# A gated recurrence with an MLP behind it: softplus and erf from their own tables in place of five table passes and a Newton step

## The chip, the cores and the metric

The kernel runs on one core of a Trainium2 chip. The metric is the device time of one execution in microseconds. Five engines work side by side, each from its own queue in order: TensorE (PE, with its weight loads listed as PEld), VectorE (DVE), ScalarE (ACT), GpSimd (POOL) and SyncE (SP, which issues the DMAs). All arithmetic is in float32.

## The reference

The core of it (4 x 8 heads, 768 steps, head size 48; then 3072 tokens, width 384, hidden width 2048):

```python
mag = np.sqrt(a_re * a_re + a_im * a_im)
scale = np.minimum(mag, 0.999) / (mag + 1e-06)
a_re_n, a_im_n = (a_re * scale, a_im * scale)
for t in range(S):
    ar, ai = (a_re_n[:, :, t, :, None], a_im_n[:, :, t, :, None])
    new_re = ar * S_re - ai * S_im
    new_im = ar * S_im + ai * S_re
    S_re, S_im = (new_re + kv, new_im)          # kv = outer(k_t, v_t)
    y[:, :, t] = np.einsum('bhd,bhde->bhe', q[:, :, t], S_re)
...
h = x @ w_in
sp = np.maximum(h, 0.0) + np.log1p(np.exp(-np.abs(h)))
g = h * erf(sp)
return (g @ w_out)
```

The weights w_in and w_out come as float64 and are narrowed on the chip.

## The kernel before, in words

The 3072 tokens are cut into 12 units of 256 tokens, two chunks of 128 each. The main loop runs u = 0 to 12. In round u four strands are emitted interleaved by `weave`, each over its own share of the round:

- **rec**: the recurrence of unit u, chunk 0 then chunk 1. The 8 heads go as two groups of 4 (hg 0 and 1). Decays, keys and queries are transposed (tiles r, k, q into PSUM tr, and on to rT, K, Q in SBUF); dg is the diagonal; then seven levels of doubling (L384 to L402). At each level and head group 4 products go into PSUM tile lv (in the trace 8 PE instructions, since a float32 product shows as two), DVE copies a part of lv into A (L389) and multiplies a half of Q by decays (L398), POOL does the same for a half of K (L400). The next level of that group needs Q and K. Two PSUM buffers serve lv. At the end of a chunk come kn, y and kv (the output and the new state), and xt, the transpose of the output into xT.
- **dec** (gate_decay): the decay r of unit u+1, a chain of 15 DVE instructions on 128 x 768 elements or more with a reciprocal (L267) in it and Square, Ln, Exp and Abs on ACT; emitted over the first fifth of the round. **ang** (gate_angle): Arctan, running sums (PSUM tile sum) and Sin, late in the round.
- **ffs**: the MLP of unit u-1, in two slabs of 8 blocks of 128 hidden features. `ff_in` puts two blocks at a time (6 products) into a PSUM tile hps of 128 x 512, of which there are two buffers. ACT copies it to h (L477) and DVE clamps it to z (L480). `softplus` makes four ACT passes over the 128 x 2048 slab: Exp, Ln(1 + .), then Ln and Exp(-.), the last two for 1 / z in tile yy. `erf_times_h` goes by quarters of 512: two DVE instructions for a Newton step on yy (L505, L506), Gelu on ACT, and two DVE instructions that turn gelu(sqrt(2) z) into h * erf(z) (L508, L509). `ff_out` sums 16 products per chunk of 128 tokens into PSUM tile ops (L519), ACT scales the result, and it goes out.
- weights, in round 0 alone.

Round 12 has only ffs. Round 11 has no dec and no ang. So rounds 1 to 10 are alike, and round 0 is the start.

What sets the order on each engine is a scheduler that goes by the emission order as priority and by its own estimate of the engines' time; buffers come from pools. `act` chains all table functions in the order of emission, and puts a table load where the next function is in another set; plain copies on ACT are outside of that chain. A PSUM tile that two engines read is read by one after the other, in the order of emission.

Of the kernel before, what the change touches and what calls it, by code (L numbers as in the profile page):

```python
# [18 lines left out]
P = 128  # L19
# [6 lines left out]
    "gelu_and_others": (AF.Gelu,),  # L26
# [4 lines left out]
def weave(*streams):  # L31
    """Emit the steps of each (begin, end, steps) evenly over its part of the window."""
    order = []
    for si, (begin, end, steps) in enumerate(streams):
        for i, step in enumerate(steps):
            order.append((begin + (end - begin) * (i + 0.5) / len(steps), si, i, step))
    for _, _, _, step in sorted(order, key=lambda e: e[:3]):
        step()
# [3 lines left out]
def kernel(  # L42
# [11 lines left out]
    """Gated linear recurrence with complex diagonal gates, then h * erf(softplus(h)) between two  # L54
    matrix products, in float32 throughout.

    A gate is r * exp(2 pi i theta). The angles enter the queries and keys once, as cosine and sine
    of their running sum (kept within half a turn), which leaves a real recurrence with decay r over
    2 * D rows. A chunk of 128 steps is solved by seven levels of doubling: at the level of blocks of
    m steps, a query in the second block of a pair meets the keys of the first, the query times the  # L60
    decays from its block's start up to it, the key times those after it up to its block's end.
    These are products of decays only, never quotients, so gates may be as small as they like,
    or zero.
    """
# [15 lines left out]
    RT2 = math.sqrt(2.0)  # L80
# [12 lines left out]
    yp = ctx.enter_context(tc.tile_pool(name="yp", bufs=1))  # L93
# [21 lines left out]
    # pair[l]: 1 where the key of the row lies in the first block of the pair of blocks of 2**l  # L115
    # whose second block the query of the column lies in.
# [58 lines left out]
    def narrow(dst, src, shape):  # L175
        """float64 from memory, as raw 64-bit words, to the nearest float32: the upper 20 bits of the
        significand with the exponent's bias changed, and the lower 32 as a number scaled by the
        power of two, added. What is under float32's normal range becomes zero."""
# [21 lines left out]
    def weights():  # L200
        """Steps that bring the weights on chip."""
# [19 lines left out]
    def gate_decay(u):  # L221
# [6 lines left out]
        def s0():  # L228
# [4 lines left out]
            # The logarithm's range; below it the decay is under 1e-13 in any case.  # L233
# [8 lines left out]
        def s2():  # L242
            # One Newton step takes 1 / sqrt(s) to full precision.
# [10 lines left out]
        def s3():  # L254
            # mag in s; 1 / ((mag + EPS) * (mag + |ar|)) in y
# [27 lines left out]
    def gate_angle(u):  # L283
        def t0():
            ar = flat(T["ar", u])
            n, hv = T["n"], T["hv"]
            # Half the angle of (|ar|, ai); turns of (ar, ai) from it.
# [174 lines left out]
    def ff_in(u, sl):  # L462
# [4 lines left out]
        def two(i):  # L467
            def f():
# [3 lines left out]
                for e in range(2):  # L472
                    f0 = (sl * SLAB + i + e) * P
                    for kd in range(KD):
                        nc.tensor.matmul(out=ps[:, e, :], lhsT=w_in_sb[:, kd, f0:f0 + P], rhs=T["xT", u][:, kd, :],  # L475
                                         start=(kd == 0), stop=(kd == KD - 1))
                nc.scalar.copy(out=T["h", u, sl][:, i:i + 2, :], in_=ps)  # L477
                # Above 8, erf(softplus(h)) is 1 in float32; below -16, 1 + exp(h) is 1 to its last place.
                # h itself stays whole.
                nc.vector.tensor_scalar(out=T["z", u, sl][:, i:i + 2, :], in0=ps, scalar1=8.0, scalar2=-16.0,  # L480
                                        op0=OP.min, op1=OP.max)
# [3 lines left out]
    def softplus(u, sl):  # L485
        def f():
            z = T["z", u, sl]
            y = yp.tile([P, SLAB, NT], FP, tag="yy", name="yy")
            act(out=z, in_=z, func=AF.Exp)
            act(out=z, in_=z, func=AF.Ln, bias=1.0)  # L490
            act(out=y, in_=z, func=AF.Ln)
            act(out=y, in_=y, func=AF.Exp, scale=-1.0)
            T["yy", u, sl] = y
        return [f]

    def erf_times_h(u, sl):
        # erf(z) = sqrt(2) * gelu(sqrt(2) * z) / z - 1; a Newton step gives -1 / z to full precision.
        n = SLAB // 4

        def part(i):  # L500
            def f():
                ss = slice(i * n, (i + 1) * n)
                h, z, y = (T[nm, u, sl][:, ss, :] for nm in ("h", "z", "yy"))
                t = yp.tile([P, n, NT], FP, tag="t", name="t")
                nc.vector.tensor_tensor(out=t, in0=z, in1=y, op=OP.mult)  # L505
                nc.vector.scalar_tensor_tensor(out=y, in0=t, scalar=-2.0, in1=y, op0=OP.add, op1=OP.mult)  # L506
                act(out=z, in_=z, func=AF.Gelu, scale=RT2)
                nc.vector.tensor_tensor(out=z, in0=z, in1=y, op=OP.mult)  # L508
                nc.vector.scalar_tensor_tensor(out=h, in0=z, scalar=1.0 / RT2, in1=h, op0=OP.add, op1=OP.mult)  # L509
            return f  # L510
        return [part(i) for i in range(SLAB // n)]
# [66 lines left out]
```

## Time and profile before

| | |
|---|---|
| time, median of 2 runs (lowest to highest) | 1558.42 us (1557.83 to 1559.02) |
| span of the profiled execution | 1557.6 us |
| PE busy | 1350.9 us (87%) |
| DVE busy | 1171.2 us (75%) |
| ACT busy | 597.6 us (38%) |
| POOL busy | 418.0 us (27%) |
| mean granted TensorE clock | 0.814 |

The profiled execution's own span is 0.8 us below the median of the runs. The granted clock is given as a share of 2.4 GHz; 0.5 is 1.2 GHz, and a mean between the two says which part of the stretch stood at each. An engine's idle time is listed with what ended it.

### The profile page before, as it was taken

How to read it: one execution, taken by the hardware profiler on the slowest of the kernel's cores; microseconds unless marked ns; L12 is line 12 of the kernel's file. 1: busy time of each engine (PE TensorE's matmuls, PEld its weight loads, DVE VectorE, ACT ScalarE, POOL GpSimd, SP SyncE). 2: the span in 40 equal slices, each digit the busy share in tenths (PEclk: the TensorE clock that was granted, in tenths of full speed). 3: DMA queues.
4: the chain of work that ended last, by engine and by line, in shares of the span. 5: the costliest groups of instructions: out<-in, count | busy, mean ns of one | idle time of the engine just before them, and what ended most of it. 6: DMA issues, size and time to landing. Idle time of an engine off the chain costs nothing.

```text
span 1557.6 us, 18736 instructions
## 1 busy us (share of the span) xinstructions
PE 1350.9 (87%) x6912; PEld 1137.9 (73%) x6912; DVE 1171.2 (75%) x2104; ACT 597.6 (38%) x751; POOL 418.0 (27%) x387
## 2 busy tenths in 40 slices
PE   0455598998998998998998998998998998999997
PEld 0244477887877787787877787887877887888784
DVE  6999979579579669579589669579589669578535
ACT  2301033443443443444443443434443443434425
POOL 4445523122123222122132222122132122132210
PEclk9997557797797886797797887797797887799888
DMA  8214100100100100100100100100100100000000
GB/s 173 90 31 114 58 11 11 31 21 11 32 21 11 31 21 11 31 21 11 32 21 11 31 21 11 31 21 11 31 21 10 31 21 0 1 11 1 0 11 10
DMA packets 131386, 42.09 MB, mean 27 GB/s; under 512 B 125408, under 2 KB 128480, under 8 KB 130528
## 3 DMA queue, kind: packets, MB, share of 16 engines
q1 hardware_dynamic: 131296, 40.90, 11.4%
q8 instruction: 55, 0.90, 0.2%
q14 instruction: 35, 0.29, 0.1%
HBM read 36.18 MB, written 4.72 MB: 26 GB/s over the span
## 4 chain that ended last, share of the span: by engine, by line
PE 60%; DVE 25%; issue 6%; ACT 6%; POOL 2%; DMA 0%; SPq 0%; DVEq 0%; ACTq 0%; POOLq 0%
PE lv L384 20%; PE ops L519 12%; PE hps L475 9%; PE y L411 4%; DVE y L267 3%; PE y L414 3%; PE tr L340 3%; PE kv L429 3%; ACT z L146 2%; DVE A L389 2%; PE dg L370 2%; DVE tot L402 2%; DVE z L480 2%; DVE Q L398 1%; POOL K L400 1%
## 5 line engine op out<-in xcount | busy, mean ns | idle before, releaser
L384 PEld LDWEIGHTS lv<-Q,K 96*128 96x128 f32 x2688 | 438.3, 246 | 158.9 <-issue 100.6
L384 PE MATMUL lv<-Q,K 96*128 96x64 f32 x2688 | 448.6, 330 | 101.5 <-DVE Q L398 90.7
L400 POOL TENSOR_TENSOR K<-K,tot 96x256 f32<-96x256 f32 x280 | 262.7, 939 | 377.0 <-PE lv L384 243.8
L475 PE MATMUL hps<-xT,w_in_sb 128*128 128x256 f32 x1152 | 305.5, 415 | 0.6 <-ACT xT L449 0.6
L519 PE MATMUL ops<-w_out_sb,h 128*128 128x384 f32 x768 | 283.6, 498 | 7.8 <-DVE z L480 6.5
L146 ACT ACTIVATE z<-z 128x2048 f32<-128x2048 f32 (+1 forms) x144 | 152.3, 1057 | 319.9 <-DVE t L505 308.6
L475 PEld LDWEIGHTS hps<-xT,w_in_sb 128*128 128x128 f32 x1152 | 232.8, 212 | 32.2 <-ACT xT L449 1.0
L400 POOL TENSOR_TENSOR K<-K,rT 96x256 f32<-96x256 f32 x48 | 74.1, 1544 | 640.5 <-PE lv L384 640.5
L389 DVE COPY_PREDICATED A<-pair,lv 128x256 f32<-128x256 uint8 x336 | 171.3, 510 | 42.1 <-PE lv L384 39.4
L519 PEld LDWEIGHTS ops<-w_out_sb,h 128*128 128x128 f32 x768 | 135.1, 192 | 71.1 <-DVE z L480 6.9
L398 DVE TENSOR_TENSOR Q<-Q,tot 96x256 f32<-96x256 f32 x280 | 150.2, 536 | 0.0
L477 ACT COPY h<-hps 128x512 f32<-128x512 f32 x96 | 55.8, 581 | 161.0 <-PE hps L475 161.0
L437 DVE TENSOR_TENSOR S<-S,kv 96x192 f32<-96x192 f32 x32 | 11.2, 350 | 133.1 <-PE kv L429 133.1
L480 DVE TENSOR_SCALAR z<-hps 128x512 f32<-128x512 f32 x96 | 65.0, 682 | 44.1 <-ACT h L477 44.1
L411 PE MATMUL y<-v,A 128*128 128x48 f32 x384 | 95.3, 354 | 0.2 <-DVE tot L402 0.2
L411 PEld LDWEIGHTS y<-v,A 128*128 128x128 f32 x384 | 84.3, 279 | 0.4 <-DVE tot L402 0.4
L426 ACT COPY kn<-kn 128x384 f32<-128x384 f32 x40 | 19.2, 479 | 165.6 <-PE kn L424 146.3
L340 PE MATMUL tr<-ident,r 128*96 128x128 f32 x192 | 49.5, 387 | 37.3 <-DVE r L278 36.5
L414 PE MATMUL y<-S,Q 96*128 96x48 f32 x320 | 81.4, 347 | 0.0
L145 ACT ACT_TABLE_LOAD x62 | 79.5, 1283 | 1.1
L505 DVE TENSOR_TENSOR t<-z,yy 128x512 f32<-128x512 f32 x96 | 71.7, 747 | 9.7 <-ACT yy L146 9.7
L506 DVE SCALAR_TENSOR_TENSOR yy<-t,yy 128x512 f32<-128x512 f32 x96 | 74.7, 778 | 0.1
(96 smaller groups left out, 1753.6 us busy)
## 6 DMA issues: line engine op xcount, KB each, us to landing
raw<-in_moe_w_in_dram SPq DMA_DIRECT2D x6, 1024.0 KB, 5.5
raw<-in_moe_w_out_dram SPq DMA_DIRECT2D x8, 768.0 KB, 4.3
ar<-in_a_re_dram SPq DMA_DIRECT2D x24, 192.0 KB, 3.2
ai<-in_a_im_dram SPq DMA_DIRECT2D x24, 192.0 KB, 3.2
q<-in_q_dram SPq DMA_DIRECT2D x24, 192.0 KB, 3.7
k<-in_k_dram SPq DMA_DIRECT2D x24, 192.0 KB, 3.3
v<-in_v_dram SPq DMA_DIRECT2D x24, 192.0 KB, 3.2
out_dram<-o SPq DMA_DIRECT2D x24, 192.0 KB, 1.9
```

What stands on the lines that cost most here:

```text
L145: in_order(nc.scalar.preload_act_table_set(sets[0]))
L146: in_order(nc.scalar.activation(func=func, **kw))
L340: nc.tensor.transpose(out=ps[0:D2, j, :], in_=src(j), identity=ident)
L384: nc.tensor.matmul(out=lv[:, j], lhsT=K[0:D2, j, :], rhs=Qv[0:D2, j, :, 1, :], start=True, stop=True)
L389: nc.vector.copy_predicated(out=halves(A, 1), mask=pair[l], data=lv.rearrange("p h b m -> p (h b) m"))
L398: nc.vector.tensor_tensor(out=halves(Q, 1)[0:D2], in0=halves(Q, 1)[0:D2], in1=over(0), op=OP.mult)
L400: nc.gpsimd.tensor_tensor(out=halves(K, 0)[0:D2], in0=halves(K, 0)[0:D2], in1=over(1), op=OP.mult)
L411: nc.tensor.matmul(out=y[:, j, :], lhsT=st["A"][:, j, :], rhs=T["v", u][:, c, hg * HG + j, :], start=True, stop=first)
L414: nc.tensor.matmul(out=y[:, j, :], lhsT=st["Q"][0:D2, j, :], rhs=T["S", hg][0:D2, j, :], start=False, stop=True)
L475: nc.tensor.matmul(out=ps[:, e, :], lhsT=w_in_sb[:, kd, f0:f0 + P], rhs=T["xT", u][:, kd, :], start=(kd == 0), stop=(kd == KD - 1))
L480: nc.vector.tensor_scalar(out=T["z", u, sl][:, i:i + 2, :], in0=ps, scalar1=8.0, scalar2=-16.0, op0=OP.min, op1=OP.max)
L519: nc.tensor.matmul(out=ps, lhsT=T["h", u, sl][:, e, jj * P:(jj + 1) * P], rhs=w_out_sb[:, i, :], start=(i == 0), stop=(i == KF - 1))
```

## The change

Softplus and Erf each have a table. hps is now copied to h by DVE, and ACT makes z = Softplus(hps) from PSUM at once, in pieces of 512. One Erf pass goes over the slab of 2048, and four DVE multiplications of 512 give h * erf(z). The clamp, the tile yy, the four slab passes, the Gelu and the Newton step are gone, and so is the scale in `ff_out`. Softplus and Erf stand in two different table sets. The line numbers of the changed kernel are lower by 1 up to its L476.

```diff
-    "gelu_and_others": (AF.Gelu,),
+    "softplus": (AF.Softplus,),
+    "sigmoid_and_others": (AF.Erf,),
...
-                nc.scalar.copy(out=T["h", u, sl][:, i:i + 2, :], in_=ps)
-                nc.vector.tensor_scalar(out=T["z", u, sl][:, i:i + 2, :], in0=ps, scalar1=8.0, scalar2=-16.0,
-                                        op0=OP.min, op1=OP.max)
+                nc.vector.tensor_copy(out=T["h", u, sl][:, i:i + 2, :], in_=ps)
+                act(out=T["z", u, sl][:, i:i + 2, :], in_=ps, func=AF.Softplus)
...
-    def softplus(u, sl):
-        def f():
-            z = T["z", u, sl]
-            y = yp.tile([P, SLAB, NT], FP, tag="yy", name="yy")
-            act(out=z, in_=z, func=AF.Exp)
-            act(out=z, in_=z, func=AF.Ln, bias=1.0)
-            act(out=y, in_=z, func=AF.Ln)
-            act(out=y, in_=y, func=AF.Exp, scale=-1.0)
...
     def erf_times_h(u, sl):
-                t = yp.tile([P, n, NT], FP, tag="t", name="t")
-                nc.vector.tensor_tensor(out=t, in0=z, in1=y, op=OP.mult)
-                nc.vector.scalar_tensor_tensor(out=y, in0=t, scalar=-2.0, in1=y, op0=OP.add, op1=OP.mult)
-                act(out=z, in_=z, func=AF.Gelu, scale=RT2)
-                nc.vector.tensor_tensor(out=z, in0=z, in1=y, op=OP.mult)
-                nc.vector.scalar_tensor_tensor(out=h, in0=z, scalar=1.0 / RT2, in1=h, op0=OP.add, op1=OP.mult)
+            h, z = T["h", u, sl], T["z", u, sl]
+            act(out=z, in_=z, func=AF.Erf)
+            for i in range(0, SLAB, 2):
+                nc.vector.tensor_tensor(out=h[:, i:i + 2, :], in0=h[:, i:i + 2, :], in1=z[:, i:i + 2, :], op=OP.mult)
...
-                nc.scalar.mul(out=o, in_=ps, mul=-RT2)
+                nc.scalar.copy(out=o, in_=ps)
...
-                ffs += ff_in(u - 1, sl) + softplus(u - 1, sl) + erf_times_h(u - 1, sl)
+                ffs += ff_in(u - 1, sl) + erf_times_h(u - 1, sl)
```

With fewer steps in ffs the emission is spread anew, and the scheduler's order changes. PE before, in chunk 0 of a round from the first level on (hps are the products of `ff_in`, lv those of the levels, 4 to a level and head group):

```order
L384 MATMUL lv<-Q,K 128x64 x4
L475 MATMUL hps<-xT,w_in_sb 128x256 x3
L384 MATMUL lv<-Q,K 128x64 x4
L475 MATMUL hps<-xT,w_in_sb 128x256 x7
L384 MATMUL lv<-Q,K 128x64 x48
L424 MATMUL kn<-ident,K 128x96 x6
```

PE now, from the same place:

```order
L383 MATMUL lv<-Q,K 128x64 x4
L474 MATMUL hps<-xT,w_in_sb 128x256 x3
L383 MATMUL lv<-Q,K 128x64 x8
L474 MATMUL hps<-xT,w_in_sb 128x256 x5
L383 MATMUL lv<-Q,K 128x64 x4
L474 MATMUL hps<-xT,w_in_sb 128x256 x7
L383 MATMUL lv<-Q,K 128x64 x8
L474 MATMUL hps<-xT,w_in_sb 128x256
L383 MATMUL lv<-Q,K 128x64 x8
L474 MATMUL hps<-xT,w_in_sb 128x256 x2
L383 MATMUL lv<-Q,K 128x64 x4
L474 MATMUL hps<-xT,w_in_sb 128x256
```

Before, 36 of the round's 48 hps products stand ahead of the last six levels, which run as one block of 48 lv, and 6 follow it in the chunk. Now 30 stand ahead of level 2 and 14 are spread from there to the end of the chunk; 4 are left for chunk 1 (before: 6).

ACT before, around the same place (s, y, n are gate_decay's, q the transposed query, h the copy of hps):

```order
L145 ACT_TABLE_LOAD
L477 COPY h<-hps 128x512
L146 ACTIVATE y<-s 128x768
L146 ACTIVATE y<-y 128x768
L146 ACTIVATE n<-y 128x768
L477 COPY h<-hps 128x512
L354 COPY K<-tr 96x512
L361 COPY q_4073<-tr 96x512
L477 COPY h<-hps 128x512
L146 ACTIVATE n<-ar 128x768
L361 COPY q_4091<-tr 96x512
L477 COPY h<-hps 128x512 x2
```

ACT now (z<-hps is Softplus, z<-z is Erf):

```order
L145 ACTIVATE z<-hps 128x512
L144 ACT_TABLE_LOAD
L145 ACTIVATE y<-s 128x768
L360 COPY q_3878<-tr 96x512
L145 ACTIVATE y<-y 128x768
L145 ACTIVATE n<-y 128x768
L360 COPY q_3896<-tr 96x512
L145 ACTIVATE n<-ar 128x768
L144 ACT_TABLE_LOAD
L145 ACTIVATE z<-hps 128x512 x3
L144 ACT_TABLE_LOAD
L145 ACTIVATE z<-z 128x2048
```

The first Softplus now stands ahead of gate_decay's Ln and the second behind its Abs, with a table load on each side. In the whole program there are 83 table loads now and 63 before; a round of the middle has 7 instead of 5.

DVE now, at gate_decay's reciprocal (before, the clamp of one hps stood just ahead of the reciprocal, and both head groups' level-0 instructions just behind it):

```order
L261 TENSOR_TENSOR hv<-hv,ai 128x768
L266 RECIPROCAL y<-y 128x768
L476 COPY h<-hps 128x512
L270 TENSOR_TENSOR hv<-hv,y 128x768
L271 TENSOR_TENSOR n<-n,y 128x768
L272 SCALAR_TENSOR_TENSOR s<-s 128x768
L388 COPY_PREDICATED A<-pair_130,lv 128x128x2
L277 TENSOR_TENSOR r<-s,n 128x1536
L397 TENSOR_TENSOR Q<-Q,tot 96x128x2
```

The level-0 instructions have moved ahead of the reciprocal, and a copy of hps stands right behind it. In both kernels level 1's Q, on which PE's level 2 waits, comes behind r.

## Rows read from the trace of the kernel before

**Rows 1.** The page: busy time per engine, and the granted clock in 40 slices.

```profile
PE 1350.9 (87%) x6912; PEld 1137.9 (73%) x6912; DVE 1171.2 (75%) x2104; ACT 597.6 (38%) x751; POOL 418.0 (27%) x387
PEclk9997557797797886797797887797797887799888
```

**Rows 2.** Windows of one round; length, busy PE, PEld, DVE, ACT, POOL, clock.

```profile
807.00:831.00 24.00, 23.70 (x126) 20.26 (x125) 19.64 (x30) 14.36 (x22) 2.29 (x2) 0.93 0.17 33
831.00:840.00 9.00, 2.33 (x19) 2.15 (x18) 9.00 (x12) 7.36 (x5) 3.27 (x2) 0.72 0.00 1
840.00:869.00 29.00, 28.52 (x130) 26.91 (x131) 21.05 (x42) 5.93 (x10) 7.29 (x10) 0.50 0.00 1
869.00:917.00 48.00, 47.66 (x270) 36.29 (x268) 36.79 (x77) 19.51 (x24) 15.91 (x14) 1.00 0.15 34
```

**Rows 3.** PE in order of time, same round: start, length, what, idle before.

```profile
827.86 3.24 PE L475 MATMUL hps<-xT,w_in_sb 128*128 128x256 f32 x14
833.17 1.99 PE L384 MATMUL lv<-Q,K 96*128 96x64 f32 x16 [2.08 <-DVE Q L398]
839.75 18.77 PE L384 MATMUL lv<-Q,K 96*128 96x64 f32 x80 [4.59 <-DVE Q L398]
...
865.31 2.04 PE L475 MATMUL hps<-xT,w_in_sb 128*128 128x256 f32 x4
...
870.53 0.49 PE L448 MATMUL xt<-ident,x 128*128 128x128 f32 x3
```

**Rows 4.** DVE in order of time, same round.

```profile
816.41 0.95 DVE L247 TENSOR_TENSOR n<-n,s 128x768 f32<-128x768 f32 x1
...
827.25 4.93 DVE L267 RECIPROCAL y<-y 128x768 f32<-128x768 f32 x1
...
837.50 1.77 DVE L278 TENSOR_TENSOR r<-s,n 128x1536 f32<-128x1536 f32 x1
```

**Rows 5.** Groups of instructions by line and shape: busy, mean ns, idle before.

```profile
L506 DVE SCALAR_TENSOR_TENSOR yy<-t,yy 128x512 f32<-128x512 f32 x96 | 74.7, 778 | 0.1
L508 DVE TENSOR_TENSOR z<-z,yy 128x512 f32<-128x512 f32 x96 | 70.3, 732 | 0.2
L509 DVE SCALAR_TENSOR_TENSOR h<-z,h 128x512 f32<-128x512 f32 x96 | 69.0, 719 | 0.1
L480 DVE TENSOR_SCALAR z<-hps 128x512 f32<-128x512 f32 x96 | 65.0, 682 | 44.1 <-ACT h L477 44.1
L146 ACT ACTIVATE z<-z 128x2048 f32<-128x2048 f32 x48 | 91.7, 1911 | 11.2 <-DVE z L480 10.8
L146 ACT ACTIVATE z<-z 128x512 f32<-128x512 f32 x96 | 60.5, 630 | 308.8 <-DVE t L505 308.6
L145 ACT ACT_TABLE_LOAD x62 | 79.5, 1283 | 1.1
```

**Rows 6.** ACT in order of time: a pass and the table load behind it.

```profile
835.20 1.91 ACT L146 ACTIVATE yy<-yy 128x2048 f32<-128x2048 f32 x1
837.12 1.28 ACT L145 ACT_TABLE_LOAD   x1
```

**Rows 7.** Round 11, which has no gate_decay: windows, then PE.

```profile
1412.00:1438.00 26.00, 22.14 (x154) 20.09 (x153) 22.97 (x42) 14.93 (x15) 10.45 (x14) 0.96 0.00 1
1438.00:1451.00 13.00, 13.00 (x66) 12.73 (x67) 4.52 (x12) 2.64 (x6) 0.00 (x0) 0.50 0.01 1
...
1428.48 2.38 PE L475 MATMUL hps<-xT,w_in_sb 128*128 128x256 f32 x10
...
1434.42 0.55 PE L424 MATMUL kn<-ident,K 96*128 96x96 f32 x4 [1.72 <-POOL K L400]
```

**Rows 8.** Round 12, the tail: PE.

```profile
1498.44 23.72 PE L475 MATMUL hps<-xT,w_in_sb 128*128 128x256 f32 x96 [0.57 <-ACT xT L449]
1528.65 13.59 PE L519 MATMUL ops<-w_out_sb,h 128*128 128x384 f32 x32 [6.49 <-DVE z L480]
1543.54 10.67 PE L519 MATMUL ops<-w_out_sb,h 128*128 128x384 f32 x32 [1.31 <-DVE h L509]
```

More of the change, by code (lines that the diff above doesn't have):

```diff
@@ L79 @@
     NSL = KF // SLAB
-    RT2 = math.sqrt(2.0)
     const = ctx.enter_context(tc.tile_pool(name="const", bufs=1))
@@ L92 @@
     zp = ctx.enter_context(tc.tile_pool(name="zp", bufs=2))
-    yp = ctx.enter_context(tc.tile_pool(name="yp", bufs=1))
     op = ctx.enter_context(tc.tile_pool(name="op", bufs=2))
@@ L476, in f, with erf_times_h @@
                                          start=(kd == 0), stop=(kd == KD - 1))
-                nc.scalar.copy(out=T["h", u, sl][:, i:i + 2, :], in_=ps)
-                nc.vector.tensor_scalar(out=T["z", u, sl][:, i:i + 2, :], in0=ps, scalar1=8.0, scalar2=-16.0,
-                                        op0=OP.min, op1=OP.max)
+                nc.vector.tensor_copy(out=T["h", u, sl][:, i:i + 2, :], in_=ps)
+                act(out=T["z", u, sl][:, i:i + 2, :], in_=ps, func=AF.Softplus)
             return f
         return [two(i) for i in range(0, SLAB, 2)]
-    def softplus(u, sl):
+    def erf_times_h(u, sl):
         def f():
-            z = T["z", u, sl]
-            y = yp.tile([P, SLAB, NT], FP, tag="yy", name="yy")
-            act(out=z, in_=z, func=AF.Exp)
-            act(out=z, in_=z, func=AF.Ln, bias=1.0)
-            act(out=y, in_=z, func=AF.Ln)
-            act(out=y, in_=y, func=AF.Exp, scale=-1.0)
-            T["yy", u, sl] = y
-        return [f]
-    def erf_times_h(u, sl):
-        n = SLAB // 4
-        def part(i):
-            def f():
-                ss = slice(i * n, (i + 1) * n)
-                h, z, y = (T[nm, u, sl][:, ss, :] for nm in ("h", "z", "yy"))
-                t = yp.tile([P, n, NT], FP, tag="t", name="t")
-                nc.vector.tensor_tensor(out=t, in0=z, in1=y, op=OP.mult)
-                nc.vector.scalar_tensor_tensor(out=y, in0=t, scalar=-2.0, in1=y, op0=OP.add, op1=OP.mult)
-                act(out=z, in_=z, func=AF.Gelu, scale=RT2)
-                nc.vector.tensor_tensor(out=z, in0=z, in1=y, op=OP.mult)
-                nc.vector.scalar_tensor_tensor(out=h, in0=z, scalar=1.0 / RT2, in1=h, op0=OP.add, op1=OP.mult)
-            return f
-        return [part(i) for i in range(SLAB // n)]
+            h, z = T["h", u, sl], T["z", u, sl]
+            act(out=z, in_=z, func=AF.Erf)
+            for i in range(0, SLAB, 2):
+                nc.vector.tensor_tensor(out=h[:, i:i + 2, :], in0=h[:, i:i + 2, :], in1=z[:, i:i + 2, :], op=OP.mult)
+        return [f]
     def ff_out(u):
```

## The prediction

> **What bounds the kernel now.** I read the page's busy row and clock row first, then windows over one middle round, then PE and DVE in order of time inside it. PE is busy for 87% of the span and DVE for 75%, but the clock row does not stay at 9: after the start it swings between 6 and 9 in each round [rows 1]. So time can be won in three ways: less PE idle time, more time at 2.4 GHz, or less PE work. The change takes no product away, so only the first two are open.
>
> The windows of the round that runs from 807 to 923 us show where both are lost [rows 2]. From 831 to 840 PE is busy for 2.33 of 9.00 us while DVE is busy for all 9.00. From 840 to 869 PE is busy for 28.52 of 29.00 us, but at a clock of 0.50. From 869 to 917 it is busy for 47.66 of 48.00 at 1.00: there PE alone is the limit, and a freer DVE buys nothing. In order of time [rows 3]: the last block of hps products ends at 831.1, PE waits 2.08 and then 4.59 us for Q from DVE, and when the levels go on at 839.75 they run 80 lv instructions in 18.77 us, 0.235 us each. Just ahead of the second wait, 16 took 1.99, 0.124 each. The clock comes back by 869, 3.7 us after hps products start again at 865.31. What holds DVE is gate_decay: from n (816.41) over the reciprocal (4.93 us) to the end of r (839.27) it goes through a queue of 22.9 us [rows 4], and Q of level 1 stands behind r.
>
> So a round of 116 us holds about 7 us of PE waiting and about 29 us at half the clock, which cost some 14 us more. Ten rounds (1 to 10) are like this.
>
> **The change, part by part.**
>
> *DVE work taken out.* The clamp (682 ns) becomes a copy of the same shape from PSUM, at the same price. The final instruction stays as a multiplication, which I price as the 732 ns row. Three of the five others go or shrink: 778 + 732 + 719 ns less per quarter [rows 5] is 2.23 us, 8 quarters to a round, 17.8 us a round and 214 us over the 24 slabs. Nearly all of it lay beside a busy PE (from 840 on, 21.05 us of DVE work in 29 us that PE filled), so I put its direct worth at nothing in the middle rounds. Its cover is PE at the low clock; were PE at 2.4 GHz there, the old DVE work would be in the way (below).
>
> *ACT.* Per slab four passes of 1911 ns and four Gelus of 630 become four Softplus of 512 and one Erf. No row shows a Softplus or an Erf; the bounds are the nearest passes, 630 ns for 512 elements and 1911 for 2048, and I take these. 20 more table loads of 1283 ns are 26 us. ACT is at 38% and ends below 30%: off the path but for two places. First, gate_decay's Ln now waits for the first Softplus and a load. The Softplus itself waits for DVE's copy of the same PSUM tile, as the clamp waited for ACT's copy (44.1 us idle, all on L477) [rows 5]. That puts n about 2 us later (0.68 + 0.63 + 1.28, less the copy that stood there). But two copies of hps, a query and two Q now come before n and not behind it, about 3 us of the queue; against this, level 0 (two pairs, about 1.7 us) comes ahead of the reciprocal, and the copy behind it. By count r ends within half a microsecond of where it did: -0.3 us. The second place is Erf of slab 2, in front of a copy of q in chunk 1: from the last hps product it takes 0.68 + 0.63 + 1.28 + 1.91 = 4.5 us plus the copy, and PE has about 5 us of ops, tr and dg to do meanwhile: +0.5 us, bounds 0 and 1.5.
>
> *PE waits in the burst.* PSUM has two hps tiles; the third copy stands behind the reciprocal, and the second Softplus behind Abs and a load. I count three waits of 2, 0.8 and 5.3 us, where there were 2.08 and 4.59. They add nothing of their own, as level 2 starts when DVE lets it; they push hps work out: 30 products are done by then and not 36.
>
> *The order of the levels.* This is the main term. Level 2 to xt took 839.75 to 870.53 = 30.8 us [rows 3], 29 of them at 0.50. At 1.00 that work is 29.0 / 2 + 1.8 = 16.3 us. Now 8 products more stand in the stretch (14 for 6), at 0.45 us each (14 instructions in 3.24 us, two to a product): +3.6, so 19.9. Is it at 1.00? The last block before level 2 is now 7 products, of which 6 follow DVE's copy behind the reciprocal without a break: 12 instructions, 5.5 us even at the low clock. At 865.31 the clock was back after 3.7 us of a mix that held fewer. And round 11 is a picture of what follows: without gate_decay its order had hps products spread between the levels, and it ran from 1412 to 1438 at 0.96 [rows 7]. It also shows two prices. PE was idle 3.9 of these 26 us, 1.72 of them waiting for POOL's K; I take 2, as 6 products stand near the end of the levels now. And its clock fell once the products had run out, 0.50 from 1438 to 1451; here two single products lie in that section, and I take 7 us at half clock, 3.5 lost. So 19.9 + 2 + 3.5 = 25.4 against 30.8: **-5.4 us**. Chunk 1 has two products fewer (-0.9) but starts at the low clock where it started at the high one (+1.5).
>
> Per round: -0.3 + 0.5 - 5.4 - 0.9 + 1.5 = -4.6 us, ten times **-46 us**. Round 11 has its spread order already: -1. In the tail [rows 8] PE waits 6.49 and 1.31 us for DVE and the first 32 ops take 13.59 us where the next take 10.67: the four passes and the Newton step of the last slab are bare there. Now the last quarter needs 0.68 + 0.63 + 1.28 + 1.91 + 0.73 = 5.2 us behind its products, and slab 1's half of the first ops lasts 10.67 / 2 = 5.3. So 6.5 + 1.3 + 2.9 = 10.7 falls away: **-10.5 us**. Round 0 and its weights are untouched.
>
> **Sum** on the profiled execution: 1557.6 - 46 - 1 - 10.5 = 1500; that execution lies 0.8 us below the median, which changes nothing: **1500 us, -3.7%**. About 2% is what a measurement of this kernel can tell from no change.
>
> **One rule against it.** The trace has 62 loads with 1.1 us of idle time before them in all [rows 5], and the load at 837.12 follows a pass that ends at 837.11 [rows 6]: 1.28 us is the whole of a switch here. The Trainium skill (ScalarE: Activation LUTs, What ACT_TABLE_LOAD costs) puts 1.38 us of draining beside the 1.28 us of the load, 2.66 us a switch, and its rule is to do all of one set before switching; the change goes the other way, with two sets to a slab. By that the two loads ahead of n and in front of the second Erf would cost 2.8 us a round more, and the sum would be 1528. The rows above do not bear that out.
>
> **The rivals.**
>
> *The clock does not come back before level 2.* The 6 products then do not lift it, single products between levels at 0.235 us an instruction do not either, and the whole stretch lasts 2 x 19.9 = 39.8 us for 30.8. With chunk 1 that is about +10 us a round: 1558 + 100 - 11 = 1647, slower by 5.7%. It decides at the block behind the reciprocal: if waits for the copy and Softplus split it. For it: the copies now stand in DVE's queue, the full engine of that stretch, and before them ACT did the same from an idle queue. Against it: the 3.7 us at 865.31, and the block of 6 in level 5, which would lift the clock by then and leave about 1580.
>
> *The low stretch only moves.* The fall comes after the spread products, in the section of y and kv, as in round 11, and lasts as long as before there and into chunk 1, or POOL's K (round 11: idle 3.9 us) limits the levels. Then rounds gain 0 to 1 us and only the tail is left: 1557.6 - 10.5 - 5 = 1542.
>
> *Better than that.* DVE is 17.8 us lighter a round, so the levels wait less than in round 11, whose DVE was busy 22.97 of 26 us, and single products carry the clock over the y section. Without the 2, 3.5, 1.5 and 0.5 us of the sum a round gains 12: 1557.6 - 121 - 12 = 1425.
>
> *A table load costs twice what the row says.* If a switch held ACT for another 1.28 us in front of the new functions, the loads ahead of n and of the second Erf would add 2.6 us to a round: 1500 + 26 = 1526. The back-to-back start in the row speaks against it. The drain that the Trainium skill gives (ScalarE: Activation LUTs, What ACT_TABLE_LOAD costs) would be such a cost.
>
> **How the numbers follow.** The forecast (1455 to 1525) gets 0.50, the better case 0.16, the one that only moves it 0.20, the clock that stays low 0.10 (in part 1580, in full 1647), the dear table load 0.04. The range leaves out the far end of the better case and the far half of the slow one: 1440 to 1565. Faster by over 2% (under 1527): 0.50 + 0.16 and a little of the rest, 0.67. Slower by over 2% (over 1590): 0.08. Within 2%: 0.25.
>
> **What would show it.** The levels at 1.00 behind the block of hps products, a mean clock of 0.85 to 0.88 (before 0.814), a round of 111 to 112 us; PE's longest wait ahead of an hps product with a Softplus as its end; DVE busy about 957 us; ops that follow the tail's hps within 1 us. It would be wrong if lv instructions between level 2 and level 6 still take 0.235 us, if r ends later than 23 us behind n's old place, or if PE waits for q copies behind Erf in chunk 1 by more than 1 us.

## The result, and the profile after

The changed kernel takes **1396.63 us** (median of 2 runs, 1395.35 to 1397.91) where the kernel before took 1558.42: a ratio of 0.896, 95% interval 0.895 to 0.898. The forecast was 1500 with a range down to 1440. The sign was right and the size was far too small: -162 us, forecast -58.

The page of the changed kernel, busy time per engine and granted clock in 40 slices [rows 1]:

```profile
PE 1198.5 (86%) x6912; PEld 990.5 (71%) x6912; DVE 988.4 (71%) x1816; ACT 436.3 (31%) x603; POOL 357.1 (26%) x387
PEclk9755557999999998999999998998998999999989
```

The number of PE instructions is the same, but they are busy for 152 us less. From slice 8 on, where the kernel before swings between 6 and 9, the clock hardly leaves 9. (The low slices in front are round 0. That the row of the kernel before has 9 there says little: round 0 took 219.6 us before and 218.3 now, and its first eight transposes 1.92 and 1.91 us.) Windows over rounds 1 to 11, and over round 11 alone, give the size; columns are length, PE, PEld, DVE, ACT, POOL, clock, DMA share, GB/s. The kernel before:

```profile
220.00:1497.00 1277.00, 1198.25 (x6325) 1015.32 (x6323) 956.94 (x1822) 531.10 (x671) 308.64 (x300) 0.81 0.09 18
1395.81:1496.57 100.76, 96.51 (x556) 82.02 (x556) 67.86 (x142) 40.27 (x49) 24.51 (x26) 0.89 0.01 5
```

The changed kernel:

```profile
218.00:1345.00 1127.00, 1052.92 (x6329) 872.38 (x6328) 789.21 (x1558) 386.26 (x537) 247.47 (x300) 0.94 0.10 21
1252.36:1344.62 92.26, 91.13 (x556) 77.18 (x556) 53.86 (x118) 23.85 (x35) 20.14 (x26) 0.94 0.02 5
```

The rounds are 150 us shorter. PE's idle time in them is 78.8 us before (1277.00 - 1198.25) and 74.1 now: only 4.7 of the 150 are less waiting. The other 145 are the same instructions in less busy time. With two levels, a mean of 0.81 puts 2 x 0.19 = 38% of the time at 1.2 GHz, some 485 us, and 0.94 puts 12% there, some 135 us. Where the busy time fell, the lines of PE show (operation, shape and count; busy us, mean ns; idle time just before them and its releasers). Before:

```profile
L384 PE MATMUL lv<-Q,K 96*128 96x64 f32 x2688 | 448.6, 330 | 101.5 <-DVE Q L398 90.7 <-DVE tot L402 4.1 <-DVE A L373 3.2
L475 PE MATMUL hps<-xT,w_in_sb 128*128 128x256 f32 x1152 | 305.5, 415 | 0.6 <-ACT xT L449 0.6
```

Now:

```profile
L383 PE MATMUL lv<-Q,K 96*128 96x64 f32 x2688 | 358.2, 284 | 54.3 <-DVE Q L397 46.6 <-DVE tot L401 4.1 <-DVE A L372 3.2
L474 PE MATMUL hps<-xT,w_in_sb 128*128 128x256 f32 x1152 | 333.6, 430 | 43.4 <-ACT z L145 42.3 <-ACT xT L448 0.6
```

The levels' products are 90 us shorter in all; the two products of y (95.3 and 81.4 us before, 74.7 and 64.5 now) are some 37 us shorter, kv 17 and ops 15. The hps products are 28 us longer, because it is now they that run at the low clock behind a wait. The waits moved with them: 44 us fewer ahead of lv for Q, 42 us more ahead of hps for Softplus.

Windows of one round, of the kind that was read before (from the xt of chunk 1 of one round to the xt of chunk 0 of the next and on) [rows 2]:

```profile
732.00:753.00 21.00, 18.86 (x115) 15.72 (x115) 17.19 (x27) 12.75 (x18) 3.68 (x3) 1.00 0.11 20
753.00:764.00 11.00, 5.69 (x16) 4.30 (x16) 11.00 (x10) 0.60 (x1) 0.73 (x1) 0.72 0.18 36
764.00:784.00 20.00, 19.67 (x151) 18.24 (x150) 14.72 (x31) 8.75 (x12) 8.31 (x10) 0.98 0.10 21
784.00:828.00 44.00, 43.58 (x246) 32.74 (x245) 27.08 (x63) 10.63 (x16) 10.26 (x14) 1.00 0.13 28
```

The 29 us at 0.50 have become 20 at 0.98, and the low clock stands in the window of the wait. PE in order of time in it (start, length, what, idle before) [rows 3]:

```profile
748.86 1.08 PE L383 MATMUL lv<-Q,K 96*128 96x64 f32 x8 [1.71 <-DVE Q L397]
749.78 2.37 PE L474 MATMUL hps<-xT,w_in_sb 128*128 128x256 f32 x10
...
753.03 0.65 PE L474 MATMUL hps<-xT,w_in_sb 128*128 128x256 f32 x2
758.98 5.49 PE L474 MATMUL hps<-xT,w_in_sb 128*128 128x256 f32 x12 [5.31 <-ACT z L145]
764.26 2.11 PE L383 MATMUL lv<-Q,K 96*128 96x64 f32 x16
766.21 0.65 PE L474 MATMUL hps<-xT,w_in_sb 128*128 128x256 f32 x2
...
779.46 1.04 PE L410 MATMUL y<-v,A 128*128 128x48 f32 x8
...
780.82 0.62 PE L474 MATMUL hps<-xT,w_in_sb 128*128 128x256 f32 x2
...
784.29 0.51 PE L447 MATMUL xt<-ident,x 128*128 128x128 f32 x3
```

The long wait is still there, 5.31 us. Behind it 12 hps instructions run at the low clock (5.49 us, 0.46 each; ahead of it 0.24 each), and with the lv at 764.26 the clock is back: 16 in 2.11 us, 0.13 each. In this round it then stays up to xt, through the products of y (8 in 1.04 us); in rounds 5, 7 and 10 it falls once more just ahead of xt, which the section on the prediction comes back to.

DVE and ACT around the wait [rows 4, 6]; DVE:

```profile
752.76 4.94 DVE L266 RECIPROCAL y<-y 128x768 f32<-128x768 f32 x1
757.62 0.62 DVE L476 COPY h<-hps 128x512 f32<-128x512 f32 x1
761.27 1.78 DVE L277 TENSOR_TENSOR r<-s,n 128x1536 f32<-128x1536 f32 x1
```

ACT:

```profile
758.33 0.60 ACT L145 ACTIVATE z<-hps 128x512 f32<-128x512 f32 x1 [9.34 <-DVE h L476]
```

The chain of the wait is reciprocal (to 757.70), copy (to 758.24), Softplus (to 758.93), hps at 758.98. The costs of the new work, from the lines by shape [rows 5]:

```profile
L144 ACT ACT_TABLE_LOAD x82 | 105.2, 1283 | 1.4
L476 DVE COPY h<-hps 128x512 f32<-128x512 f32 x96 | 64.6, 673 | 32.3 <-PE hps L474 32.2
L486 DVE TENSOR_TENSOR h<-h,z 128x512 f32<-128x512 f32 x96 | 61.9, 686 | 15.9 <-ACT z L145 15.9
L145 ACT ACTIVATE z<-hps 128x512 f32<-128x512 f32 x96 | 57.4, 598 | 240.7 <-DVE h L476 240.1
L145 ACT ACTIVATE z<-z 128x2048 f32<-128x2048 f32 x24 | 45.9, 1912 | 0.3
```

PE in the tail [rows 8]:

```profile
1346.49 18.41 PE L474 MATMUL hps<-xT,w_in_sb 128*128 128x256 f32 x72 [0.57 <-ACT xT L448]
1366.26 5.45 PE L474 MATMUL hps<-xT,w_in_sb 128*128 128x256 f32 x24 [1.36 <-ACT z L145]
1371.55 5.32 PE L495 MATMUL ops<-w_out_sb,h 128*128 128x384 f32 x16
1377.07 15.75 PE L495 MATMUL ops<-w_out_sb,h 128*128 128x384 f32 x48 [0.20 <-DVE h L486]
```

### The profile page after: what moved, and what is told of

It reads as the page before. It is cut to its first block, busy times and chain, and to the rows that moved or that the text cites. A ratio compares the mean times of both kernels' runs of the same rounds, so it can differ in the third digit from the quotient of the medians.

```text
span 1396.2 us, 18332 instructions
## 1 busy us (share of the span) xinstructions
PE 1198.5 (86%) x6912; PEld 990.5 (71%) x6912; DVE 988.4 (71%) x1816; ACT 436.3 (31%) x603; POOL 357.1 (26%) x387
## 5 line engine op out<-in xcount | busy, mean ns | idle before, releaser
L383 PEld LDWEIGHTS lv<-Q,K 96*128 96x128 f32 x2688 | 359.3, 205 | 97.6 <-POOL K L399 34.2
L383 PE MATMUL lv<-Q,K 96*128 96x64 f32 x2688 | 358.2, 284 | 54.3 <-DVE Q L397 46.6
L474 PE MATMUL hps<-xT,w_in_sb 128*128 128x256 f32 x1152 | 333.6, 430 | 43.4 <-ACT z L145 42.3
L399 POOL TENSOR_TENSOR K<-K,tot 96x256 f32<-96x256 f32 x280 | 219.4, 785 | 481.4 <-issue 223.8
L145 ACT ACTIVATE z<-hps 128x512 f32<-128x512 f32 x96 | 57.4, 598 | 240.7 <-DVE h L476 240.1
L476 DVE COPY h<-hps 128x512 f32<-128x512 f32 x96 | 64.6, 673 | 32.3 <-PE hps L474 32.2
L410 PE MATMUL y<-v,A 128*128 128x48 f32 x384 | 74.7, 289 | 0.2 <-DVE tot L401 0.2
L486 DVE TENSOR_TENSOR h<-h,z 128x512 f32<-128x512 f32 x96 | 61.9, 686 | 15.9 <-ACT z L145 15.9
L401 DVE TENSOR_TENSOR tot<-tot 96x128 f32<-96x128 f32 (+5 forms) x280 | 66.0, 254 | 7.6
L413 PE MATMUL y<-S,Q 96*128 96x48 f32 x320 | 64.5, 285 | 0.0
L410 PEld LDWEIGHTS y<-v,A 128*128 128x128 f32 x384 | 61.9, 208 | 0.5 <-DVE tot L401 0.4
```

What stands on the lines that cost most here:

```text
L383: nc.tensor.matmul(out=lv[:, j], lhsT=K[0:D2, j, :], rhs=Qv[0:D2, j, :, 1, :], start=True, stop=True)
L399: nc.gpsimd.tensor_tensor(out=halves(K, 0)[0:D2], in0=halves(K, 0)[0:D2], in1=over(1), op=OP.mult)
L401: nc.vector.tensor_tensor(out=nt[0:D2], in0=tv[:, :, 0], in1=tv[:, :, 1], op=OP.mult)
L410: nc.tensor.matmul(out=y[:, j, :], lhsT=st["A"][:, j, :], rhs=T["v", u][:, c, hg * HG + j, :], start=True, stop=first)
L413: nc.tensor.matmul(out=y[:, j, :], lhsT=st["Q"][0:D2, j, :], rhs=T["S", hg][0:D2, j, :], start=False, stop=True)
L476: nc.vector.tensor_copy(out=T["h", u, sl][:, i:i + 2, :], in_=ps)
```

## The experiments

The change does two things: it takes work from DVE and ACT, and it gives ffs fewer steps, on which the scheduler builds another order, on all engines. **Theory "order"**: the gain is the new places of the hps products, which keep PE's clock up; the lighter engines matter little by themselves. **Rival "work"**: the gain is DVE's and ACT's lighter load, and the clock follows from shorter waits. Eleven kernels were run. The numbers, with rounds 1 to 11 by windows as above (edges to the microsecond; the columns on the rounds are of the one run that was profiled):

| kernel | median us | ratio to before (95%) | PE busy in rounds | PE idle in rounds | clock in rounds |
|---|---|---|---|---|---|
| before | 1558.42 | 1 | 1198 | 79 | 0.81 |
| changed | 1396.63 | 0.896 (0.895 to 0.898) | 1053 | 74 | 0.94 |
| 1 old work, new steps | 1436.76 | 0.920 (0.916 to 0.924) | 1060 | 101 | 0.93 |
| 2 new work, old steps | 1533.91 | 0.984 (0.983 to 0.986) | 1179 | 85 | 0.84 |
| 3 changed, old DVE load in place | 1525.21 | 0.979 (0.977 to 0.980) | 1135 | 118 | 0.87 |
| 4 changed, same load in chunk 1 | 1443.80 | 0.928 (0.925 to 0.931) | 1105 | 76 | 0.90 |
| 5 before, a product per level | 1664.11 | 1.068 (1.066 to 1.069) | 1334 | 47 | 0.83 |
| 6 before, a block | 1557.40 | 1.000 (0.999 to 1.001) | 1223 | 51 | 0.84 |
| 7 before, block and products | 1575.31 | 1.011 (1.009 to 1.012) | 1246 | 46 | 0.86 |
| 8 the same with other data | 1576.10 | 1.012 (1.010 to 1.013) | 1245 | 47 | 0.86 |
| 9 changed, a block | 1490.02 | 0.956 (0.954 to 0.958) | 1154 | 65 | 0.89 |
| 10 changed, gate_decay later | 1401.78 | 0.899 (0.896 to 0.901) | 1089 | 45 | 0.91 |
| 11 changed, h copied by ACT | 1345.24 | 0.861 (0.855 to 0.867) | 1045 | 38 | 0.94 |

**1. The old work in the new steps.** The kernel before, with softplus and erf_times_h of a slab emitted as one step, so that ffs has the few steps of the changed kernel:

```diff
-                ffs += ff_in(u - 1, sl) + softplus(u - 1, sl) + erf_times_h(u - 1, sl)
+                tail = softplus(u - 1, sl) + erf_times_h(u - 1, sl)
+                ffs += ff_in(u - 1, sl) + [lambda fs=tail: [f() for f in fs]]
```

> The old activation in full (five table passes and the Newton step), but its passes of one slab emitted as one step, so that ffs has 12 steps as in the changed kernel. In the order that comes of it hps products stand between the levels again (44 lv of a chunk in pieces of 4 to 12 with 1 to 6 products between) and not 36 ahead of one block of 48. Theory O (the order keeps the clock up, DVE's work was beside it): 1400 to 1450 us, the levels of chunk 0 at a clock of 0.9 or more. Rival W (the 17.8 us of DVE work per round taken out are what counts): about 1558, 1530 at best.

1436.76 us: -121.5 of the change's -162, with all the old passes on ACT and the Newton step on DVE. PE in order of time, in one of its rounds:

```profile
779.00 1.94 PE L384 MATMUL lv<-Q,K 96*128 96x64 f32 x8 [5.49 <-DVE Q L398]
780.74 4.67 PE L475 MATMUL hps<-xT,w_in_sb 128*128 128x256 f32 x12
785.24 1.90 PE L384 MATMUL lv<-Q,K 96*128 96x64 f32 x16
```

The clock falls in the wait for Q, 12 hps instructions stand behind it, and the levels that follow run at 0.12 us an instruction. The old order has no hps there. So it goes in nine of the rounds 1 to 10; in round 4, with the same order, the clock falls again among the levels (see the end of the next section). The order is of the new kind, but not that of the changed kernel: 24 lv instructions follow the block where that has 16 and then hps.

**2. The new work in the old steps.** The changed kernel, with empty steps in place of those that went away:

```diff
-                ffs += ff_in(u - 1, sl) + erf_times_h(u - 1, sl)
+                ffs += ff_in(u - 1, sl) + [lambda: None] + erf_times_h(u - 1, sl) + 3 * [lambda: None]
```

> The new activation in full (Softplus, Erf, one multiplication), with four empty steps per slab, so that ffs has 20 steps as before. The order then has one block of 44 lv with no product in it in chunk 0, as before, and 103 table loads. Theory O: the block runs at 0.5 again, most of the gain is lost: 1500 to 1550 us. Rival W: within 2% of the changed kernel, 1380 to 1425.

1533.91 us: -24.4 for all the work that was removed. The levels are a block again, at the low clock, 0.22 us an instruction:

```profile
732.13 12.18 PE L383 MATMUL lv<-Q,K 96*128 96x64 f32 x56 [0.43 <-DVE Q L397]
```

The two parts by themselves give 121.5 and 24.4, together 162: the order carries most of it. What part of the order, PE's or that of DVE and ACT, these two runs can't tell. On top of the new order the old work costs the rounds 34 us (1161 - 1127), and PE's idle time is 27 longer; that price is rough, since 14 us lie in the one round of experiment 1 in which the clock fell.

**3. The new order with DVE's old load.** The changed kernel with three more DVE instructions for each quarter of 512, on a scratch tile, ahead of the multiplication:

```diff
+                nc.vector.tensor_tensor(out=t, in0=z[:, i:i + 2, :], in1=h[:, i:i + 2, :], op=OP.mult)
+                nc.vector.scalar_tensor_tensor(out=t, in0=t, scalar=-2.0, in1=z[:, i:i + 2, :], op0=OP.add, op1=OP.mult)
+                nc.vector.tensor_tensor(out=t, in0=t, in1=h[:, i:i + 2, :], op=OP.mult)
```

> The changed kernel with three more DVE instructions of 512 per quarter, whose result nobody reads, so that DVE has the old load again. The order on PE is nearly that of the changed kernel. Theory O: 1397 to 1430 us (at most 1 to 3 us a round for DVE in the way). Rival W: the gain goes back with the work, 1500 or more.

1525.21 us: 128 of the 162 us are lost, which speaks against "order" alone. PE shows how (second kind of round):

```profile
729.62 1.00 PE L384 MATMUL lv<-Q,K 96*128 96x64 f32 x8
732.77 0.55 PE L424 MATMUL kn<-ident,K 96*128 96x96 f32 x4 [2.15 <-POOL K L400]
...
740.64 1.48 PE L429 MATMUL kv<-v,kn 128*96 128x48 f32 x8
...
749.70 3.78 PE L475 MATMUL hps<-xT,w_in_sb 128*128 128x256 f32 x8 [1.07 <-ACT z L146]
```

The levels run at 2.4 GHz, then PE waits 2.15 us and once more 0.81 us for POOL's K, with no hps product placed in the section of y, and from 735.0 on the section runs at 1.2 GHz until the hps at 749.70 (kv, 8 in 1.48 us; in the changed kernel 0.84). On DVE the added instructions run among the last levels, up to 737.0, and the copies that free hps come only behind the updates of S, which wait for kv, at 743.03 and 748.27. But the scheduler moved PE's order too, from the sixth of the seven levels on, so the run doesn't hold the order fixed: it shows what the load costs together with the order that comes of it, not what it costs under an order that stays.

**4. The same load elsewhere.** 24 DVE multiplications of 512 a round on a spare tile, over the second half of each round:

```diff
+        extra = [lambda: nc.vector.tensor_tensor(out=spare, in0=spare, in1=spare, op=OP.mult)] * (24 if u > 0 else 0)
-        weave((0.0, 1.0, rec), (0.0, 0.2, dec), (0.0, 0.85, ffs), (0.75, 0.95, ang), (0.0, 0.9, wts))
+        weave((0.0, 1.0, rec), (0.0, 0.2, dec), (0.0, 0.85, ffs), (0.75, 0.95, ang), (0.0, 0.9, wts), (0.5, 1.0, extra))
```

> The changed kernel with 24 DVE multiplications of 512 more per round on a spare tile, spread over the second half of the round, so that DVE has the old load again but not in the queue of chunk 0's last levels. PE's order stays nearly that of the changed kernel. If DVE's load as such is what counts: 1500 or more, as with the added instructions beside the multiplications (1525). If what counts is where it stands, since there it held up the copies of hps and so the products of the y section: 1400 to 1430.

1443.80 us, between the two ranges: the load costs 47 us here and 128 ahead of the multiplication. In the profiled run (1452.87, the longest of the four; the others are 1442.86 to 1443.91) PE's idle time is 76 us, as in the changed kernel, and its busy time 52 us longer. So even here the load is paid for in clock. PE's order moved here too, in round 6 from the first level on; that the place of the load decides its price fits both runs and is not shown apart from the order.

**5. A product per level on the kernel before.** Tile lv gets a second half, and one product of 256 columns, which nothing reads, goes ahead of each level's products:

```diff
-                lv = ps_lv.tile([P, HG, nb, m], FP, tag="lv", name="lv")
+                both = ps_lv.tile([P, 2, HG * nb * m], FP, tag="lv", name="lv")
+                lv = both[:, 0, :].rearrange("p (h b m) -> p h b m", h=HG, m=m)
+                if u > 0:
+                    nc.tensor.matmul(out=both[:, 1, :], lhsT=ident, rhs=w_in_sb[:, 0, 0:256], start=True, stop=True)
```

> The kernel before with one product more per level and head group from round 1 on, 128 x 256 into the unused half of the level's PSUM tile, which nobody reads: 28 products or some 12 us of PE work at 2.4 GHz more per round, and nothing else. Theory O, in its part on the clock (products between the levels hold it up): the block of levels runs at 1.0 instead of 0.5, wins 14 to 22 us a round and pays 12: 1450 to 1550 us, in spite of the added work, with lv at about 0.12 us an instruction. If the clock has nothing to do with what stands between the levels: 1558 + 130 to 250, 1690 or more.

1664.11 us, between the two ranges. Single products among the levels don't bring the clock back: through the block the lv stay at 0.23 us an instruction and the added pair takes 1.17 us.

```profile
890.24 1.81 PE L387 MATMUL lv<-Q,K 96*128 96x64 f32 x8
891.84 1.17 PE L385 MATMUL lv<-w_in_sb,ident 128*128 128x256 f32 x2
```

**6. A block on the kernel before.** The same tile, six such products in one piece, in chunk 0 ahead of level 1 of the second head group:

```diff
+                for _ in range(6 if u > 0 and c == 0 and l == 1 and hg == 1 else 0):
```

> The kernel before with six products of 128 x 256 more in chunk 0 of each round from round 1, in one piece ahead of level 1 of head group 1, where PE waits for DVE anyway; nobody reads them. The run with one product more per level showed that sparse products do not bring a fallen clock back. Theory O2 (a block of products lifts the clock, as the six hps products behind the reciprocal did at 759 us of the changed kernel, and products between the levels are then needed to hold it): the levels begin at 1.0 and fall to 0.5 on the way, as nothing stands between them: 1500 to 1550 us. Rival K (once up, levels alone hold it): all 40 lv at 0.12 us, 1400 to 1440. Rival N (the block does not lift it): 1560 to 1620.

1557.40 us over 10 runs: nothing, to a tenth of a per cent. The idle time falls by 28 us, the busy time rises by 25: the block fills a wait and pays for itself, and the mean clock only goes from 0.81 to 0.84. In the round that begins at 801 us the clock does hold through the wait that is left (2.57 us, then 16 lv in 1.97 us), and falls among the levels behind it (64 in 15.54).

**7. Both.** The block, and a product for each level and head group from level 2 on, in chunk 0:

```diff
+                for _ in range(0 if u == 0 or c == 1 else 6 if l == 1 and hg == 1 else 1 if l > 1 else 0):
```

> The same block of six and, in chunk 0 alone, one product per level and head group from level 2 on (10 a round): 16 products or about 7 us of PE work at 2.4 GHz that nobody reads. Theory O2: the levels run at 1.0 from end to end, 14 us a round won and about 5 paid (the block lies in a wait): 1440 to 1490 us, faster than before with more work on PE and the same on DVE and ACT. Rival K: like the run without the ten, and slower than it by some 40. Rival W (DVE's work is the limit there): no more than 1530.

1575.31 us, where theory O2 had 1440 to 1490. This is the nearest copy of the new order that was tried in the kernel before, and it does not do it:

```profile
836.27 2.81 PE L385 MATMUL lv<-w_in_sb,ident 128*128 128x256 f32 x12
...
842.47 1.08 PE L387 MATMUL lv<-Q,K 96*128 96x64 f32 x8 [1.84 <-DVE Q L401]
...
845.92 1.81 PE L387 MATMUL lv<-Q,K 96*128 96x64 f32 x8
```

The block runs at 2.4 GHz and so do the lv behind the wait (8 in 1.08 us); some 2 us later, with PE busy all the while, the clock falls and stays down for the rest of the levels.

**8. Other data.** As 7, but the stationary operand is weights and not the identity (`lhsT=w_in_sb[:, 1, 0:P]`), in case products with mostly zeros counted for less.

> The run with the block of six and ten products more per round in the kernel before, with one edit: the added products multiply w_in's weights (stationary and moving) and not an identity by weights; the shapes, the order and the waits are the same. In the identity run the block brought the clock back, and it fell again among the levels in spite of the single products. If what is multiplied matters to the clock: the levels stay at 1.0, 1440 to 1500 us. If not (spacing and PE's waits decide): within 1% of that run, 1565 to 1590.

1576.10 us against 1575.31, the intervals overlap: identity or weights as the stationary operand makes no difference here.

**9. The block on the changed kernel.** Six products of weights in the same place, to shorten the wait of 5.31 us that remained:

```diff
+                for _ in range(6 if u > 0 and c == 0 and l == 1 and hg == 1 else 0):
+                    nc.tensor.matmul(out=both[:, 1, :], lhsT=w_in_sb[:, 1, 0:P], rhs=w_in_sb[:, 0, 0:256], start=True, stop=True)
```

> The changed kernel with six products of weights more (128 x 256, nobody reads them) in chunk 0 of each round, in the place in front of level 1 of head group 1 where PE then waits 5 us for Softplus. If the low clock behind that wait costs what its rows say (a block of 12 hps instructions in 5.5 us that takes 2.7 at 1.0): 1365 to 1390 us. If the added 2.7 us of PE work delay the levels, or the order that the scheduler makes of it is worse: 1397 to 1430.

1490.02 us, 93 us slower than the changed kernel: a miss. PE:

```profile
812.13 4.41 PE L477 MATMUL hps<-xT,w_in_sb 128*128 128x256 f32 x12 [2.76 <-ACT z L145]
816.68 1.97 PE L386 MATMUL lv<-Q,K 96*128 96x64 f32 x16
...
824.56 1.81 PE L386 MATMUL lv<-Q,K 96*128 96x64 f32 x8
```

The wait did shrink, to 2.76 us, and the levels began at 2.4 GHz. Then the clock fell in the middle of them, in every one of rounds 1 to 10, as in experiment 7, though here the products among them are hps as in the changed kernel. The order is not quite that of the changed kernel: 24 lv instructions follow the block of 12 hps where that has 16, and the hps behind them lie elsewhere. PE's idle time in the rounds is 9 us shorter, its busy time 101 us longer; the added instructions, 132 at 0.24 us, are some 31 of these. How much of the rest is the shorter wait and how much the moved order is not shown.

**10. gate_decay later.** `(0.0, 0.2, dec)` becomes `(0.3, 0.75, dec)` in the changed kernel.

> The changed kernel with gate_decay emitted over 0.3 to 0.75 of the round and not the first fifth, so that the reciprocal falls beside other work and hps copies do not queue behind it in one piece. PE's waits of 1.7 and 5.3 us in chunk 0, and the low clock that follows them, should shrink: 1330 to 1385 us. If the burst only moves (the same waits in front of ops or the levels of chunk 1): 1390 to 1410.

1401.78 us, 5 more than the changed kernel. PE waits 29 us less and is busy 36 us longer, at 0.91 instead of 0.94: what the waits gave back, the clock took elsewhere. Chunk 0 of a round takes 47.0 to 52.8 us where it took 52.2 to 58.1, chunk 1 takes 49.6 to 55.6 where it took 45.8 to 50.9.

**11. ACT copies h.** In the changed kernel the copy of hps goes back to ACT, ahead of Softplus on the same engine:

```diff
-                nc.vector.tensor_copy(out=T["h", u, sl][:, i:i + 2, :], in_=ps)
+                nc.scalar.copy(out=T["h", u, sl][:, i:i + 2, :], in_=ps)
```

> The changed kernel with the copy of hps to h back on ACT, ahead of Softplus, so that no hps tile waits for DVE's queue behind the reciprocal. The scheduler then puts all 48 hps products into chunk 0 (16 of them in one piece in gate_decay's stretch) and ops between the levels behind it. If DVE's queue in front of the PSUM tiles is what makes PE wait 5.3 us: 1330 to 1380 us. If ACT's longer queue (two reads of each hps tile, table loads between) makes PE wait instead: 1395 to 1430.

1345.24 us (two runs at 1334.36 and 1337.23, two at 1353.25 and 1353.48, of which the first was profiled), which beats both kernels: 3.7% below the changed one. hps no longer waits for the reciprocal on DVE:

```profile
741.07 6.69 PE L474 MATMUL hps<-xT,w_in_sb 128*128 128x256 f32 x30
749.35 4.15 PE L474 MATMUL hps<-xT,w_in_sb 128*128 128x256 f32 x18 [0.75 <-ACT z L145]
753.33 1.90 PE L383 MATMUL lv<-Q,K 96*128 96x64 f32 x16
```

All 48 hps products of the round fall into chunk 0, 24 of them in two pieces in front of the levels where PE used to wait. PE's idle time in the rounds halves (74 to 38 us) at the same clock: here the gain in the profiled run is waiting.

## Why the prediction was wrong

The forecast's mechanism held: the levels run at the high clock behind a block of hps products, and that is the gain. What failed is the size of its main term, from level 2 to xt: the forecast took two prices into it from round 11 of the kernel before, 2 us for POOL's K and 3.5 us for a low clock in the section of y, and let chunk 1 start at the low clock; in the round that was read neither price nor the low start came. Of the 9.6 us a round by which the forecast fell short (14.2 measured, 4.6 forecast) 5.4 lie there, 3.7 in chunk 1 and 0.5 in that one round stood for ten.

| term | forecast us | measured us |
|---|---|---|
| rounds 1 to 10 | -46 | -142.1 |
| round 11 | -1 | -8.5 |
| tail | -10.5 | -9.5 |
| round 0 | 0 | -1.3 |
| sum | -57.5 | -161.4 |

*The main term, level 2 to xt.* The forecast took 19.9 us for the work at 2.4 GHz, 2 for waiting on POOL and 3.5 for a low clock in the section of y, 25.4 for 30.8. Measured: 764.26 to 784.29, 20.0 us. The 19.9 was right, the 2 and the 3.5 did not come in this round: the longest wait there is 0.33 us, and single hps products at 780.82 and 783.22 stood in the section of y, which stayed at 2.4 GHz. Both prices were taken from round 11 of the kernel before [rows 7], whose DVE was busy for 88% of that stretch; in the changed kernel it is 74% (14.72 of 20.00). This is the mechanism of the rival "better than that", and the time lies below even its 1425. Experiment 3 shows the same section with the DVE load put back: both prices come, 2.15 us for POOL's K and the low clock after it. Since PE's order moved there too, that the lighter DVE kept them away is likely and not shown alone.

The read round flatters the kernel a little. In rounds 5, 7 and 10 the clock does fall just ahead of xt, and level 2 to xt takes 23.5 to 24.2 us; rounds 1, 2, 4 and 8, with the same products there, take 21.6 to 21.8. Rounds 4 and 7 have one order on PE:

```profile
578.91 0.84 PE L428 MATMUL kv<-v,kn 128*96 128x48 f32 x8
...
887.75 1.48 PE L428 MATMUL kv<-v,kn 128*96 128x48 f32 x8
```

*Chunk 1.* It was to lose 0.6 and wait 0.5 more for Erf, since it would start at the low clock. It starts at the high one and takes 50.2 us where it took 52.8: -2.6 against +1.1. Two products fewer are 0.9 of that; from its first y to its xt it takes 7.4 us for 9.2, since the clock now falls only in the last kv there.

*One round for ten.* The round that was read gained 13.7 us (116.1 to 102.4). The rounds come in three kinds by the unit's place in its batch, and the one read has the shortest chunk 0, without the state's products (y from S). By their means the kinds went from 116.2 to 102.6, from 120.9 to 106.2 and from 114.7 to 100.4 us. The mean over all is -14.2, where the forecast had -4.6.

*Round 11* "has its spread order already: -1". It gained 8.5 us: idle 4.3 to 1.1 us, clock 0.89 to 0.94. It was limited by DVE, which the forecast had read (22.97 of 26 us) and used for the prices of other rounds, and not for a gain in this one.

*DVE's work at nothing.* Under the old order that is near: experiment 2 gives 24 us in all, 10 of them in the tail (from the last xt, 61.0 to 50.8 us). Under the new order it is wrong, as the forecast's own half sentence on PE at 2.4 GHz had it: some 34 us in the rounds (experiment 1 against the changed kernel, with the reserves made there).

What was right: the waits in the burst (2 and 5.3 counted; 1.71 and 5.31 measured; the 0.8 between them did not show), 12 instructions at the low clock in 5.5 us (5.49), level 2 at 32.2 us behind xt where it was 32.6 (-0.4, forecast -0.3), and the tail, but for a wait of 1.36 us for Softplus among its hps (the forecast's three terms add to 10.7, and it wrote 10.5). The prices: Softplus 598 ns for 630, Erf 1912 for 1911, copy 673 for 682, multiplication 686 for 732. DVE is busy for 988 us, 957 forecast. The mean clock is 0.89, just above the 0.85 to 0.88 that was named; a round is 100 to 109 us and not 111 to 112.

The rivals: *the clock does not come back* fell, in 5.49 us it did. *The low stretch only moves* fell for the changed kernel, where it moves in three rounds and in part; experiments 3, 9 and 10 are kernels in which it does move. *A table load costs twice* fell: 82 loads with 1.4 us of idle time ahead of them in all, and the load at 738.21 ends 0.02 us before the next pass starts at 739.51. The Trainium skill (ScalarE: Activation LUTs, What ACT_TABLE_LOAD costs) has 2.66 us for a switch; this trace shows the 1.28 us of the load and no draining beside it.

What stays open is when the clock falls. Experiments 5 to 9 show that it is not the choice of identity or weights, that sparse products don't lift it, and that a block which keeps it up through a wait can be followed by a fall among the levels. Nor does the order on PE settle it. Rounds 4 and 7 of experiment 1 have one order and the same wait for Q (5.48 and 5.49 us); behind it the same lv run at 1.2 GHz in round 4 and at 2.4 in round 7:

```profile
556.07 1.94 PE L384 MATMUL lv<-Q,K 96*128 96x64 f32 x8 [5.48 <-DVE Q L398]
...
567.74 1.81 PE L384 MATMUL lv<-Q,K 96*128 96x64 f32 x8
...
895.45 1.00 PE L384 MATMUL lv<-Q,K 96*128 96x64 f32 x8
```

Chunk 0 is 67.6 us in the one and 53.8 in the other. So the new order lets the levels run at 2.4 GHz, in nine of ten rounds there, and does not make sure of it. What decides between two rounds of one order no run here shows, and no rule is drawn.

## What to carry to other kernels

An edit that changes the number of steps which a scheduler interleaves is two edits, and the order may be the larger: run the old work in the new steps and the new work in the old ones before a gain is put down to the arithmetic. On PE, ask of an order where the dense products stand relative to the waits and the short products, and read a stretch's clock before its idle time, in more than one round, since one order can run at either clock. Before one round is multiplied by their number, read one of each kind, and don't carry a price from a stretch whose limiting engine the change relieves.

## What the runs showed of the hardware

PE can be busy all the time and still drop to 1.2 GHz: in experiment 7 at about 845 us, some 2 us behind a wait and with 64-column products and single 256-column ones in a row. A fall inside a wait cost the changed kernel little: the 12 hps instructions behind it took 5.49 us where 12 at 2.4 GHz take 2.8, and the clock was back. A fall among the levels lasted until the next dense block, over 20 us in experiment 7. The kernel in which such a wait was shortened (experiment 9) had the fall among the levels and was 93 us slower, some 31 of them for the added instructions.

The mean clock that an execution records is a rough measure: seven executions of the kernel before, beside experiment 1, have 0.788 to 0.842 with times of 1556.3 to 1559.5 us. The readings above rest on lengths of the same instructions and on windows within one execution.
